# Attention, experts and a gated matrix product on one core: tiles at multiples of 64 bytes, an earlier split of w_out, and three loads that move

## The chip, the cores and the metric

The kernel runs on one core of a Trainium2 chip. The metric is device time in microseconds (us). The kernel before was run three times: 1268.51, 1266.70 and 1268.42 us, median 1268.42.

## The reference, cut to what matters

```python
# attention: 4 batches, 8 heads, 576 rows, 64 wide; keys and values pooled by 8
attn = softmax(scale * q @ mean8(k).T);  x = attn @ mean8(v)      # x: 2304 x 512
# experts: all 4 for every row, weighted by p
for e in range(4):
    out += p[:, e] * (relu(x @ w1[e]) @ w2[e])                    # w1: 512 x 1024, w2: 1024 x 512
# gated product
a, b = x @ w1, x @ w2                                             # x is the experts' out
h = (a * b) @ w3;  result = h @ w_out                             # w3: 1024 x 1024, w_out: 1024 x 512
```

All is in fp32. The kernel splits every operand of a large product into a high and a low part (`hi_lo`, L115: ScalarE copies the rounded high part, VectorE or GpSimd subtracts it) and makes each product from three matmuls (`mm3`, L110: lines 111, 112, 113).

## The kernel before

**Stages.** A lead-in and the attention share the first 200 us with the first expert. Then come the experts: 4 experts by 6 blocks of 384 rows by 8 slices of the hidden width, 192 units. A unit makes one slice of the hidden layer, `expert_h` (12 matmuls "g1", x moves over w1), and two units later (LAG = 2) that slice's share of the output (12 matmuls "g2", the slice `hh`, `hl` moves over w2). After the last slice of a block, `accumulate` multiplies the four sums with p on VectorE and adds them on GpSimd.

**The w3 stage** uses the same loop with 24 more units, numbered n = 0 to 23 in `made` (blocks of 3, 3 and 2 row tiles by 8 slices). It multiplies w3 with w_out beforehand, so that the last stage needs one product. `w3_h` takes a slice of w3 from the stream and splits it into the same tiles `hh`, `hl` (here the stationary operand), and 9 (in the last block 6) matmuls of 512 columns move w_out over it. `keep_w34` splits the sums at the end of a block. Between the units `made` prepares the next stage: `weights_of(j, 0)` and `(j, 1)` make the seven combinations of the gate weights of column block j, `prepare_x` those of the rows of batch 0, `put_away` stores these operands in DRAM.

**The last stage** goes twice ("halves" of the width) over 4 batches. For each of four j, `gated_rows` makes seven products of 12 matmuls of 288 columns and multiplies the two results; then 4 or 5 row tiles of 12 matmuls each go over the kept w3 w_out ("w34"). The operand of a batch has two slots, kc = 0 and 1. In the second half they are loaded from DRAM (`fetch_x`), kc = 0 into a spare slot during the products, kc = 1 (`next_x(1, first)`, L1019) into the slot that the products have just read. At the swap of the halves (`swap`: first half, batch 3) four new `weights_of` are made, two at L975 before the w34 tiles and two between them.

**What sets the order.** All is issued by hand in program order, and each engine and the one DMA queue (SP's) work in that order. `Stream` holds four raw tiles and issues a load when one is taken; `take` and `split` block SP until the raw tile is free. In the w3 stage the stream carries w_out, w3 and the gate weights, in the order written in `stream_last`.

```python
822  n = key[0] * FC + fc
823  if n + 3 < FC: stream.split(nc.vector)             # w_out, slices 3 to 7
831  if n in (7, 10, 13, 16): weights_of((n - 7) // 3, 0)
833  if n in (8, 11, 14, 17): weights_of((n - 8) // 3, 1)
837  if n in (9, 15): prepare_x(n // 15, slot(), kept_d[0][n // 15])
```

The first three slices of w_out are split at the end of the last expert block (L817 to 820), since `wo` shares the pool "z", which takes the place of the experts' tiles.

**Addresses.** Tiles lie in two stacks, from the left and from the right end of each partition. In the program before, the right stack ends 32 bytes past a multiple of 64. The tiles `hh`, `hl` (also as w3's) and `xo` (the batch operand's regular slots) are in the right stack and begin 32 bytes past a multiple of 64. The tiles of x, w1, w2, w34, z (w_out, the gated rows `g`, and the spare slots, which go under the name g too) and of the gate weights (`wh`, `wl`) are in the left one and begin at multiples of 64.

Of the kernel before, what the change touches and what calls it, by code (L numbers as in the profile page):

```python
# [17 lines left out]
def fused_kernel(  # L18
# [21 lines left out]
    nc = tc.nc  # L40
# [40 lines left out]
    xpool = experts.enter_context(tc.tile_pool(name="xpool", bufs=NB))  # L81
    w1pool = experts.enter_context(tc.tile_pool(name="w1pool", bufs=FC))
    ppool = ctx.enter_context(tc.tile_pool(name="ppool", bufs=1, side="right"))
    hpool = ctx.enter_context(tc.tile_pool(name="hpool", bufs=LAG + 1, side="right"))
    dpool = ctx.enter_context(tc.tile_pool(name="dpool", bufs=1, space=bass.MemoryType.DRAM))
    ps_q = ctx.enter_context(tc.tile_pool(name="ps_q", bufs=1, space=PSUM))
# [177 lines left out]
    with tc.manual_schedule():  # L264
# [225 lines left out]
        def probs():  # L490
            sp = ap.tile([P, NTILE], F32, tag="sp", name="sp", bufs=1)
            nc.vector.tensor_reduce(sp, dp, axis=AX.X, op=ALU.add)
            nc.vector.tensor_scalar(sp, sp, 1e-9, None, op0=ALU.add)
            nc.vector.reciprocal(sp, sp)
            nc.vector.tensor_tensor(dp, dp, sp.unsqueeze(2).broadcast_to([P, NTILE, E]), op=ALU.mult)
# [78 lines left out]
        def load_p(e, i):  # L574

            pb = ppool.tile([P, TPB, P], F32, tag="p", name="p")
            rows = p_d.rearrange("(t e) s -> e t s", e=E)[e, i * TPB:(i + 1) * TPB]
            nc.sync.dma_start(pb, rows.unsqueeze(0).broadcast_to([P, TPB, P]))
            p_t[e, i] = pb.rearrange("p t s -> p (t s)")
# [49 lines left out]

        parts = {}  # L630

        def weights_of(j, n=None):

            def split(src, at, m, eng):
                src = src.rearrange("p a b c -> p (a b c)") if len(src.shape) == 4 else src.rearrange("p a c -> p (a c)")
                hi_lo(*(t[:, at:at + m].rearrange("p a b c -> p (a b c)") for t in wop_t[j]), src, eng)

            if n != 1:
                (left, _), (right, _) = stream.take(2)
                wop_t[j] = tuple(late["wops"].tile([P, 7, 2, P], F32R, tag=t, name=t) for t in ("wh", "wl"))  # L640
                s = parts[j] = late["small"].tile([P, 4, 2, P], F32, tag="t", name="s", bufs=1)
                sub, add = ALU.subtract, ALU.add
                nc.vector.tensor_tensor(s[:, 0], right[:, :2], right[:, 2:], op=add)
                nc.vector.tensor_tensor(s[:, 1], s[:, 0], left[:, :2], op=sub)
                nc.vector.tensor_tensor(s[:, 2], left[:, :2], right[:, :2], op=sub)
                nc.vector.tensor_tensor(s[:, 3], left[:, 2:], s[:, 1], op=sub)
                split(left, A11, 2, nc.vector)
                split(right[:, 2:], A22, 1, nc.vector)
                stream.fill()
            if n != 0:  # L650
                split(parts.pop(j), S1, 4, nc.gpsimd)
# [15 lines left out]
        def prepare_x(kc, to, keep, n=None):  # L667

            (bh, th), (bl, tl) = to
            if n in (None, 0):  # L670
                r = xr_t.pop(kc)
                t = late["small"].tile([P, 4, HB], F32, tag="t", name="t", bufs=1)
                sub = ALU.subtract
# [17 lines left out]
        def put_away():  # L691
            for f in stores:
                f()
            stores.clear()
# [63 lines left out]
        def enter_wide():  # L758

            experts.close()  # L760
            for name, bufs in (("z", FC), ("wops", NJ), ("small", 1)):
                late[name] = ctx.enter_context(tc.tile_pool(name=name, bufs=bufs, reuse_waits="tile"))

        def enter_operands():
            assert rounding.finished()
            later.close()
            late["xo"] = ctx.enter_context(tc.tile_pool(name="xo", bufs=4, side="right", reuse_waits="tile"))

# [26 lines left out]
        def made(u):  # L795

            kind, key, fc = u
            if kind == "e":
                e, i = key
                if e == 0 and i == 0:  # L800
                    if fc + LAG < FC:
                        stream.split(nc.vector)
                    stream.split()
                if i == NB - 1 and e < E - 1:
                    stream.split()
# [4 lines left out]
                if e == E - 1:  # L810
# [6 lines left out]
                    if i == NB - 1 and fc == FC - 1:  # L817
                        enter_wide()
                        for _ in range(3):
                            stream.split(nc.vector)  # L820
            else:
                n = key[0] * FC + fc
                if n + 3 < FC:
                    stream.split(nc.vector)
                if n == LAG + 1:
                    store_acc(NB - 1)
                if n == LAG + 2:
                    enter_operands()
                    for kc in range(2):
                        load_x(acc_d, 0, kc)  # L830
                if n in (7, 10, 13, 16):
                    weights_of((n - 7) // 3, 0)
                if n in (8, 11, 14, 17):
                    weights_of((n - 8) // 3, 1)
                if n in (13, 19):
                    put_away()
                if n in (9, 15):
                    prepare_x(n // 15, slot(), kept_d[0][n // 15])

# [32 lines left out]
        def stream_last():  # L872
            def make(fc):
                def dst():
                    t = late["z"].tile([P, 2, 1, DM], F32R, tag="z", name="wo")
                    wo_t[fc] = t[:, 0], t[:, 1]
                    return wo_t[fc]
                stream.add([late["wo"][fc]], (1, DM), dst)

            for fc in range(3):  # L880
                make(fc)
            for n, (b, fc) in enumerate((b, fc) for b in range(len(w3_blocks)) for fc in range(FC)):
                t0, rn = w3_blocks[b]
                stream.add([late["w3"][fc * P:(fc + 1) * P, t0 * P:(t0 + rn) * P]], (1, rn * P), rn)
                if n + 3 < FC:
                    make(n + 3)
                if n in (7, 10, 13, 16):
                    add_gates(0, (n - 7) // 3)

# [33 lines left out]

        half_d = [dpool.tile([P, DM], F32, tag=f"half{t}", name=f"half{t}") for t in range(NTILE)]
        z_t = [late["z"].tile([P, 2, S], F32R, tag="z", name="g") for _ in range(FC)]
        g_t = z_t[:NJ]
# [21 lines left out]
        for half in range(2):  # L948
            for b in range(B):
# [22 lines left out]
                lead_in = S % P if b % 2 else 0  # L972
                tiles = []
                if swap:
                    weights_of(0)  # L975
                    weights_of(1)
                first = b * S - (S % P if b % 2 else 0)
                if b % 2:
                    tiles.append((first // P, lambda j: edge[:, j]))
                for m in range(S // P):  # L980
# [36 lines left out]
                earlier(1)  # L1017
                first, second = xo_t[0], xo_t[1]
                next_x(1, first)  # L1019
                if half == 0 and b < B - 2:  # L1020
# [50 lines left out]
```

## Time and profile before

| | |
|---|---|
| three runs | 1268.51, 1266.70, 1268.42 us |
| the profiled execution's own time | 1272.72 us |
| its span, first to last instruction | 1271.0 us |
| mean granted TensorE clock | 0.981 of full |
| w3 stage, from its first to the last stage's first matmul | 910.22 to 975.33 us |
| swap of the halves, first matmul that waits | 1120.22 us |

The profile is one execution with each instruction's start and duration. "PE" is TensorE's matmuls; their durations overlap, so the distance between starts tells the pace. "DVE" is VectorE, "ACT" ScalarE, "POOL" GpSimd, "SPq" the issuing of DMAs. In brackets stands how long the engine had been idle and what released it.

### The profile page before, as it was taken

What the parts mean: (1) busy time and instruction counts of PE and PEld (TensorE: products, weight loads), DVE (VectorE), ACT (ScalarE), POOL (GpSimd) and SP (SyncE); (2) the same over time, 40 slices, a digit from 0 to 9 for tenths busy, and PEclk for the clock granted to TensorE, in tenths of its full rate; (3) what the DMA queues carried; (4) which work ended last, traced back from release to release, by engine and by line L of the source; (5) the groups of instructions that cost most, each with busy time, mean ns of one, the idle gap of its engine ahead of it and who ended that gap; (6) DMA issues with size and microseconds to landing.
All of it is one profiled execution on the core that took longest, in us unless ns stands there. A gap on an engine that the chain in (4) does not pass through costs nothing.

```text
span 1271.0 us, 18785 instructions
## 1 busy us (share of the span) xinstructions
PE 1222.8 (96%) x7089; PEld 1166.4 (92%) x7089; DVE 663.6 (52%) x1497; ACT 276.3 (22%) x535; POOL 358.5 (28%) x424
## 2 busy tenths in 40 slices
PE   6899999999999999999999999999978999989997
PEld 5788898999999999999999999999856999979996
DVE  4777544444445456444443544444465777655453
ACT  3343331122111113111113111111343333221010
POOL 4574410034122236212216421212121222331121
PEclk9799999999999999999999999999988999989999
DMA  7753201143112235222124322222355343755531
GB/s 178 184 161 109 57 7 57 44 129 104 56 46 57 57 98 148 57 57 57 55 59 131 93 72 78 73 77 87 112 166 186 120 181 139 256 199 196 210 136 66
DMA packets 147758, 138.47 MB, mean 109 GB/s; under 512 B 48524, under 2 KB 114644, under 8 KB 147668
## 3 DMA queue, kind: packets, MB, share of 16 engines
q1 hardware_dynamic: 147668, 137.28, 35.2%
q8 instruction: 55, 0.90, 0.3%
q14 instruction: 35, 0.29, 0.1%
HBM read 96.05 MB, written 41.19 MB: 108 GB/s over the span
## 4 chain that ended last, share of the span: by engine, by line
PE 88%; DMA 4%; DVE 4%; issue 1%; POOL 1%; SPq 1%; ACT 1%; DVEq 0%; POOLq 0%; ACTq 0%
PE g L111 24%; PE g L112 23%; PE g L113 23%; PE s L111 5%; PE s L112 5%; PE s L113 5%; PE x_ps L445 1%; PE sc L399 1%; PE at_ps L433 1%; DMA raw<-gate 1%; DMA xol<-kept 1%; DMA stxl<-in_v_dram 1%; DMA raw<-wo 0%; DVE kp L331 0%; DMA stxh<-in_q_dram 0%
## 5 line engine op out<-in xcount | busy, mean ns | idle before, releaser
L571 DVE SCALAR_TENSOR_TENSOR hhl<-g,hhh 128x384 fp32r<-128x384 f32 x192 | 106.6, 556 | 369.3 <-ACT hhh L570 369.2
L111 PE MATMUL g<-xl,w1h 128*128 128x384 f32 x768 | 263.6, 343 | 1.0 <-DVE xl L117 1.0
L111 PE MATMUL g<-hhl,w2h 128*128 128x384 f32 x768 | 262.4, 342 | 0.2 <-DVE part L590 0.2
L113 PE MATMUL g<-hhh,w2h 128*128 128x384 f32 x768 | 260.0, 339 | 0.0
L112 PE MATMUL g<-hhh,w2l 128*128 128x384 f32 x768 | 260.0, 339 | 0.0
L112 PE MATMUL g<-xh,w1l 128*128 128x384 f32 x768 | 259.8, 338 | 0.0
L113 PE MATMUL g<-xh,w1h 128*128 128x384 f32 x768 | 259.2, 338 | 0.0
L570 ACT ACTIVATE hhh<-g 128x384 fp32r<-128x384 f32 x192 | 94.7, 493 | 589.9 <-PE g L113 539.8
L223 POOL TENSOR_TENSOR dtmp<-dtmp 128x256 f32<-128x256 f32 x80 | 58.9, 736 | 412.5 <-DVE dtmp L222 367.0
L111 PEld LDWEIGHTS g<-xl,w1h 128*128 128x128 f32 x768 | 145.2, 189 | 6.0 <-DVE xl L117 2.3
L111 PEld LDWEIGHTS g<-hhl,w2h 128*128 128x128 f32 x768 | 144.1, 188 | 4.9 <-issue 4.0
L112 PEld LDWEIGHTS g<-xh,w1l 128*128 128x128 f32 x768 | 145.5, 189 | 0.0
L113 PEld LDWEIGHTS g<-xh,w1h 128*128 128x128 f32 x768 | 145.2, 189 | 0.0
L113 PEld LDWEIGHTS g<-hhh,w2h 128*128 128x128 f32 x768 | 144.2, 188 | 0.0
L112 PEld LDWEIGHTS g<-hhh,w2l 128*128 128x128 f32 x768 | 144.1, 188 | 0.0
L117 POOL TENSOR_TENSOR g<-c,g 128x576 fp32r<-128x576 f32 x32 | 47.5, 1484 | 206.4 <-ACT g L116 206.4
L591 POOL TENSOR_TENSOR acc<-acc,part 128x384 f32<-128x384 f32 x72 | 71.0, 1020 | 103.7 <-DVE part L590 103.7
L111 PE MATMUL s<-xol,wh 128*128 128x288 f32 x308 | 92.0, 299 | 6.3 <-DMA xol<-kept 6.3
L112 PE MATMUL s<-xoh,wl 128*128 128x288 f32 x308 | 91.9, 298 | 0.0
L113 PE MATMUL s<-xoh,wh 128*128 128x288 f32 x308 | 90.6, 294 | 0.0
L111 PEld LDWEIGHTS s<-xol,wh 128*128 128x128 f32 x308 | 58.3, 189 | 7.3 <-DMA xol<-kept 6.8
L113 PEld LDWEIGHTS s<-xoh,wh 128*128 128x128 f32 x308 | 58.8, 191 | 0.0
(137 smaller groups left out, 1756.0 us busy)
## 6 DMA issues: line engine op xcount, KB each, us to landing
raw<-in_moe_w_dram SPq DMA_DIRECT2D x64, 256.0 KB
din<-in_moe_w_dram SPq DMA_DIRECT2D x64, 256.0 KB
p<-p SPq DMA_DIRECT2D x24, 192.0 KB
acc<-acc SPq DMA_DIRECT2D x6, 768.0 KB
xr<-acc SPq DMA_DIRECT2D x16, 288.0 KB
half<-ob SPq DMA_DIRECT2D x18, 256.0 KB
half<-half SPq DMA_DIRECT2D x18, 256.0 KB
out_dram<-half SPq DMA_DIRECT2D x18, 256.0 KB
```

The lines of the kernel that those rows point to most:

```text
L111: nc.tensor.matmul(ps, lh, rl, start=first, stop=False)
L112: nc.tensor.matmul(ps, ll, rh, start=False, stop=False)
L113: nc.tensor.matmul(ps, lh, rh, start=False, stop=last)
L117: (lo_eng or nc.vector).tensor_tensor(lo, src, hi.bitcast(F32), op=ALU.subtract)
L223: nc.gpsimd.tensor_tensor(a, a, b, op=ALU.add)
L399: nc.tensor.matmul(sc[off:off + n, (hp % 2) * W:(hp % 2 + 1) * W], qT[:, hp, off:off + n], kT_t[b][:, hp * W:(hp + 1) * W], start=True, st ...
L433: nc.tensor.transpose(pt[:NK, g * P:(g + 1) * P], e[:, half * G + g, :], ident)
L445: nc.tensor.matmul(px[a * D:(a + 1) * D, off:off + n], vp_t[b][:NK, 2 * hp + a], at_t[i, hp // 2][:NK, 2 * (hp % 2) + a, off:off + n], sta ...
L570: nc.scalar.activation(hh, ps, AF.Relu)
L571: nc.vector.scalar_tensor_tensor(hl, ps, 0.0, hh.bitcast(F32), op0=ALU.max, op1=ALU.subtract)
L591: nc.gpsimd.tensor_tensor(acc_t[i][:, c], acc_t[i][:, c], part, op=ALU.add)
```

## The change

- `ppool`'s tile and `sp` get 8 more floats, of which the kernel uses none. The right stack's tiles then begin at multiples of 64.
- `w1pool` moves from the left to the right stack (`firsts`) and lives on through the w3 stage. The eight slices of w_out are split into its tiles, one in each unit of the last expert block (`stream.split()`, low part on GpSimd), as w1's tiles come free.
- "z" is opened after the w3 stage, on the right; `xo` moves to the left.
- The gate weights of the first half leave the stream. `load_gates(j)` loads them into tiles of tag "c" at n = 1, 6, 12, 17.
- `weights_of(j, 0)` stands at n = 5, 11, 16, 19, `weights_of(j, 1)` at 6, 12, 18, 20. `prepare_x` goes in three pieces at n = 7, 8, 10 and 13, 14, 15; `load_x` moves from n = 4 to 0, `put_away` from 13, 19 to 14, 18.
- The scratch tag "t" has two buffers instead of one.
- `next_x(1, first)` stands ahead of the swap's `weights_of(0)`, and so also ahead of `earlier(0)`, `earlier(1)` (the loads of the first half's sums).

```diff
-    w1pool = experts.enter_context(tc.tile_pool(name="w1pool", bufs=FC))
+    firsts = ctx.enter_context(ExitStack())
+    w1pool = firsts.enter_context(tc.tile_pool(name="w1pool", bufs=FC, side="right"))
-            sp = ap.tile([P, NTILE], F32, tag="sp", name="sp", bufs=1)
+            sp = ap.tile([P, NTILE + 8], F32, tag="sp", name="sp", bufs=1)[:, :NTILE]
-            pb = ppool.tile([P, TPB, P], F32, tag="p", name="p")
+            pb = ppool.tile([P, TPB * P + 8], F32, tag="p", name="p")[:, :TPB * P].rearrange("p (t s) -> p t s", s=P)
+        def load_gates(j):
+            gate_t[j] = [late["small"].tile([P, KC, P], F32, tag="c", name="gate", bufs=3) for _ in gates_d]
+            for r, d in zip(gate_t[j], gates_d):
+                nc.sync.dma_start(r, d[:, j * P:(j + 1) * P].rearrange("(k p) f -> p k f", p=P))
-                (left, _), (right, _) = stream.take(2)
+                left, right = gate_t.pop(j) if j in gate_t else (r for r, _ in stream.take(2))
-                s = parts[j] = late["small"].tile([P, 4, 2, P], F32, tag="t", name="s", bufs=1)
+                s = parts[j] = late["small"].tile([P, 4, 2, P], F32, tag="t", name="s", bufs=2)
-            late["xo"] = ctx.enter_context(tc.tile_pool(name="xo", bufs=4, side="right", reuse_waits="tile"))
+            late["xo"] = ctx.enter_context(tc.tile_pool(name="xo", bufs=4, reuse_waits="tile"))
-                if i == NB - 1 and e < E - 1:
+                if i == NB - 1:
                     stream.split()
...
-                        for _ in range(3):
-                            stream.split(nc.vector)
...
+                if n == 0:
+                    for kc in range(2):
+                        load_x(acc_d, 0, kc)
...
+        early = {n: [lambda j=j: load_gates(j)] for j, n in enumerate((1, 6, 12, 17))}
+        for j, (one, two) in enumerate(((5, 6), (11, 12), (16, 18), (19, 20))):
+            early.setdefault(one, []).append(lambda j=j: weights_of(j, 0))
+            early.setdefault(two, []).append(lambda j=j: weights_of(j, 1))
+        for kc, steps in enumerate(((7, 8, 10), (13, 14, 15))):
...
+        for n in (14, 18):
+            early[n].append(put_away)
...
+            for fc in range(FC):
+                add_rows(late["wo"][fc], w1pool, "w1", wo_t, fc)
+            for t0, rn in w3_blocks:
+                for fc in range(FC):
+                    stream.add([late["w3"][fc * P:(fc + 1) * P, t0 * P:(t0 + rn) * P]], (1, rn * P), rn)
...
+        firsts.close()
+        late["z"] = ctx.enter_context(tc.tile_pool(name="z", bufs=FC, side="right", reuse_waits="tile"))
...
+                first, second = xo_t[0], xo_t[1]
+                next_x(1, first)
                 if swap:
                     weights_of(0)
                     weights_of(1)
...
                 earlier(0)
                 earlier(1)
-                first, second = xo_t[0], xo_t[1]
-                next_x(1, first)
```

## Rows read from the trace of the kernel before

**Rows 1.** The page's first section: the span.

```profile
span 1271.0 us, 18785 instructions
```

**Rows 2.** The page's chain that ended last, shares of the span by engine.

```profile
PE 88%; DMA 4%; DVE 4%; issue 1%; POOL 1%; SPq 1%; ACT 1%; DVEq 0%; POOLq 0%; ACTq 0%
```

**Rows 3.** Busy time by stretch; columns: length, PE, PEld, DVE, ACT, POOL, clock, DMA.

```profile
400.00:500.00 100.00, 100.00 (x570) 100.00 (x569) 50.95 (x126) 19.91 (x38) 35.34 (x36) 1.00 0.35 89
910.22:975.33 65.11, 51.55 (x192) 39.34 (x193) 40.03 (x72) 26.66 (x49) 13.86 (x8) 0.84 0.62 204
911.59:914.96 3.37, 3.37 (x9) 2.48 (x8) 2.96 (x5) 1.04 (x2) 2.78 (x3) 0.50 0.10 31
915.22:928.57 13.35, 13.35 (x58) 10.73 (x57) 4.27 (x9) 3.72 (x8) 0.00 (x0) 1.00 0.88 283
938.38:942.31 3.93, 3.92 (x9) 3.17 (x10) 3.90 (x9) 1.56 (x4) 0.00 (x0) 0.50 0.16 50
962.90:966.20 3.30, 3.29 (x8) 2.62 (x9) 1.91 (x4) 0.93 (x3) 1.19 (x1) 0.50 0.39 132
997.68:1008.63 10.95, 10.95 (x50) 9.01 (x49) 10.32 (x16) 4.55 (x9) 4.10 (x4) 1.00 0.03 6
1120.20:1126.66 6.46, 6.04 (x23) 5.70 (x24) 1.76 (x5) 1.56 (x3) 2.36 (x1) 0.50 1.01 365
```

**Rows 4.** Timeline of PE: first matmul of two g1 groups and the g2 between.

```profile
895.07 0.34 PE L111 MATMUL g<-xl,w1h 128*128 128x384 f32 x1
...
897.17 0.34 PE L111 MATMUL g<-hhl,w2h 128*128 128x384 f32 x1
...
899.29 0.34 PE L111 MATMUL g<-xl,w1h 128*128 128x384 f32 x1
```

**Rows 5.** Groups by line and shape, whole span: count, busy us, mean ns, idle before.

```profile
L113 PE MATMUL s<-xoh,wh 128*128 128x288 f32 x308 | 90.6, 294 | 0.0
L113 PE MATMUL s<-g,wh 128*128 128x288 f32 x140 | 41.6, 297 | 0.0
L117 POOL TENSOR_TENSOR w2l<-raw,w2h 128x512 fp32r<-128x512 f32 x32 | 41.2, 1294 | 14.7 <-ACT w2h L116 11.2 <-issue 3.3 <-POOL kb L332 0.2
L117 DVE TENSOR_TENSOR w3hl<-raw,w3hh 128x256 fp32r<-128x256 f32 x8 | 3.4, 422 | 7.5 <-ACT w3hh L116 7.5
```

**Rows 6.** Timeline of PE: the w3 stage's three stops, where it goes on.

```profile
910.22 0.48 PE L111 MATMUL g<-wo,w3hh 128*128 128x512 f32 x1 [2.30 <-DVE part L590]
...
938.39 0.80 PE L111 MATMUL g<-wo,w3hh 128*128 128x512 f32 x1 [6.68 <-DVE w34l L117]
...
962.91 0.80 PE L111 MATMUL g<-wo,w3hh 128*128 128x512 f32 x1 [4.80 <-DVE w34l L117]
```

**Rows 7.** Timeline of VectorE ahead of the first two stops.

```profile
908.92 0.69 DVE L117 TENSOR_TENSOR wo<-raw,wo 128x512 fp32r<-128x512 f32 x1 [1.01 <-ACT wo L116]
...
927.96 0.43 DVE L643 TENSOR_TENSOR s<-raw 128x256 f32<-128x256 f32 x1 [4.17 <-DMA raw<-gate]
...
930.37 3.18 DVE L117 TENSOR_TENSOR w3hl<-raw,w3hh 128x384 fp32r<-128x384 f32 x2
933.48 0.45 DVE L674 TENSOR_TENSOR t<-xr 128x288 f32<-128x288 f32 x1
...
937.66 1.88 DVE L117 TENSOR_TENSOR w34l<-g,w34h 128x512 fp32r<-128x512 f32 x3
```

**Rows 8.** Timeline of GpSimd at the same time.

```profile
930.68 2.45 POOL L117 TENSOR_TENSOR wl<-s,wh 128x1024 fp32r<-128x1024 f32 x1 [16.31 <-ACT wh L116]
```

**Rows 9.** Timeline of the DMA queue at the swap of the halves.

```profile
1105.18 7.00 SPq L136 DMA_DIRECT2D raw<-gate  x4
1112.27 0.93 SPq L699 DMA_DIRECT2D xoh<-kept  x2
```

**Rows 10.** Timeline of PE at the swap.

```profile
1114.06 0.29 PE L113 MATMUL s<-g,wh 128*128 128x288 f32 x1
1120.22 0.61 PE L111 MATMUL s<-xol,wh 128*128 128x288 f32 x1 [5.87 <-DMA xol<-kept]
```

More of the change, by code (lines that the diff above doesn't have):

```diff
@@ L628, in fused_kernel @@
         B11, B21, B22, T1, T2, T3, T4 = range(7)
-        parts = {}
+        parts, gate_t = {}, {}
+        def load_gates(j):
+            gate_t[j] = [late["small"].tile([P, KC, P], F32, tag="c", name="gate", bufs=3) for _ in gates_d]
+            for r, d in zip(gate_t[j], gates_d):
+                nc.sync.dma_start(r, d[:, j * P:(j + 1) * P].rearrange("(k p) f -> p k f", p=P))
         def weights_of(j, n=None):
@@ L671, in prepare_x @@
                 r = xr_t.pop(kc)
-                t = late["small"].tile([P, 4, HB], F32, tag="t", name="t", bufs=1)
+                t = late["small"].tile([P, 4, HB], F32, tag="t", name="t", bufs=2)
                 sub = ALU.subtract
@@ L760, in enter_wide @@
             experts.close()
-            for name, bufs in (("z", FC), ("wops", NJ), ("small", 1)):
+            for name, bufs in (("wops", NJ), ("small", 1)):
                 late[name] = ctx.enter_context(tc.tile_pool(name=name, bufs=bufs, reuse_waits="tile"))
@@ L818, in made @@
                         enter_wide()
-                        for _ in range(3):
-                            stream.split(nc.vector)
             else:
                 n = key[0] * FC + fc
-                if n + 3 < FC:
-                    stream.split(nc.vector)
+                if n == 0:
+                    for kc in range(2):
+                        load_x(acc_d, 0, kc)
                 if n == LAG + 1:
@@ L828, in made, with piece @@
                     enter_operands()
[L829 to L838, printed above, removed]
+                for f in early.get(n, ()):
+                    f()
+        early = {n: [lambda j=j: load_gates(j)] for j, n in enumerate((1, 6, 12, 17))}
+        for j, (one, two) in enumerate(((5, 6), (11, 12), (16, 18), (19, 20))):
+            early.setdefault(one, []).append(lambda j=j: weights_of(j, 0))
+            early.setdefault(two, []).append(lambda j=j: weights_of(j, 1))
+        places = {}
+        for kc, steps in enumerate(((7, 8, 10), (13, 14, 15))):
+            for m, n in enumerate(steps):
+                def piece(kc=kc, m=m):
+                    if m == 0:
+                        places[kc] = slot()
+                    prepare_x(kc, places[kc], kept_d[0][kc], m)
+                early.setdefault(n, []).append(piece)
+        for n in (14, 18):
+            early[n].append(put_away)
         def met(u):
@@ L872, in stream_last @@
         def stream_last():
[L873 to L888, printed above, removed]
+            for fc in range(FC):
[3 more added lines that the diff above has]
+                    stream.add([late["w3"][fc * P:(fc + 1) * P, t0 * P:(t0 + rn) * P]], (1, rn * P), rn)
         hs, pss = {}, None
@@ L976, in fused_kernel @@
                     weights_of(1)
-                first = b * S - (S % P if b % 2 else 0)
                 if b % 2:
-                    tiles.append((first // P, lambda j: edge[:, j]))
+                    tiles.append(((b * S - S % P) // P, lambda j: edge[:, j]))
                 for m in range(S // P):
```

## The prediction, made before the changed kernel was run

> **What bounds the kernel now.** The page's chain comes first: of 1271.0 us [rows 1] TensorE holds 88% [rows 2]. So an edit pays only where it lets TensorE stand less, run at the higher clock, or issue its matmuls closer. The stretches say where that is possible [rows 3]. From 400 to 500 us, amid the experts, PE is busy throughout at clock 1.00, with 570 matmuls: nothing stands there, only the pace could change. The w3 stage, 910.22 to 975.33, is another matter: 192 matmuls in 65.11 us, of which PE is busy 51.55, at a mean clock of 0.84. The timeline of PE shows the large stops and who ended them [rows 6]: 2.30 us until VectorE's first expert product was through, 6.68 and 4.80 us until it had split the block's sums (`w34l`). After each, PE issues at half the pace with clock 0.50 (the 1.2 GHz level) for 3.37, 3.93 and 3.30 us [rows 3]. The one other large stop is the swap of the halves: 5.87 us until the operand had landed [rows 10], then 6.46 us at 0.50 [rows 3].
>
> **Why VectorE was late.** Its timeline has the cause [rows 7]. It works in program order, and what PE waits for is queued behind work that is due much later. Before the first stop it stands at a split of w_out whose data came late (908.92). Before the second it waits 4.17 us for gate weights, until 927.96; then come `weights_of` (2.4 us, 927.96 to 930.37), two splits of w3 (3.18), the whole of `prepare_x` (4.2 us, 933.48 to 937.66), and only then the `w34l` that frees PE's banks. The third stop repeats this with n = 15, 16 and 17.
>
> **The w3 stage, term by term.** It takes 2.30 + 65.11 = 67.4 us. Its matmuls alone: in the undisturbed stretch 915.22 to 928.57, 57 start (the 58th row began before it), so one each 234 ns; the w34 tiles, also 512 columns, start 48 in 10.95 us, one each 228 ns [rows 3]. In the first the stationary operand is off the multiple of 64, in the second it is on it. Nothing else that I see sets them apart, so I take 228 after the change: 192 x 0.228 = 43.8 us. At 234 it would be 44.9; this edit is worth 0 to 1.2 us.
>
> Stop one: no split of w_out is left ahead of the expert products. Their banks are complete one after the other while PE still works on the last slice, so VectorE follows close behind, and w3's first slices were loaded in the last expert block. I take 0 for the stop, at most 1.2.
>
> Stops two and three: n = 7 and 9 now have no more than 2.4 us of preparation each. A unit takes PE 9 x 0.228 = 2.1 us and `w3_h` runs two units ahead, so a piece of 2.4 us fits into the lead. I take 0 at n = 9. From n = 16 the blocks have two tiles and a unit lasts 1.4 us. There VectorE has two pieces of 2.4, one of 1.9 (`w34l`) and five splits of w3 of 0.42 [rows 5]: 8.8 us, while PE does units 14 to 18 in 2 x 2.1 + 3 x 1.4 = 8.4 and the lead is short. I take 1.7 us of stop, between 0 and 4.8 (today's).
>
> The DMA queue: `load_x` and `load_gates` now come early and stand between the loads of w3, and `load_gates(1)` to `(3)` make SP wait for a tile of the `weights_of` before. `put_away` (2 MB) comes at n = 14 and 18, ahead of the last slices of w3. Each raw tile is asked for three units ahead, 6 us in the first blocks and 4 us in the last. I take 1.5 us for the last slices, between 0 and 6.
>
> Sum: 43.8 + 1.7 + 1.5 = 47.0 us, so 67.4 - 47.0 = **20.4 us** saved, which holds if the short stops do not pull the clock down; one such stretch costs half of 3.3 to 3.9 us [rows 3].
>
> **The last expert block** takes over eight splits: a copy on ScalarE and 1.29 us on GpSimd each [rows 5], one in a unit of 24 matmuls, 4.2 us [rows 4]. ScalarE must wait for the first load, a few us, with the next slice's `hh` behind it; the lead of two units, 8.4 us, hides that. If it did not, PE would stand for the rest. I take 0, at most 3 us.
>
> **The swap.** SP sends the operand's load at 1112.27, behind four gate loads that it began to send at 1105.18 and that took it 7.00 us, since they wait for raw tiles [rows 9]. It lands 8 us later [rows 10]. Sent first, it can go when the last product has read its slot, ahead of the 60 w34 matmuls of 0.228, thus 13.7 us before 1114.06. It then lands near 1108.4 and the stop is gone, with its slow stretch: 5.87 + 6.46 / 2 = **9.1 us**. The gate loads go out behind it, and the second buffer of "t" lets VectorE prepare the next `weights_of` while GpSimd works on the last. What could be late next is these weights: the third is needed two `gated_rows` later, and four took 22.35 us, 975.33 to 997.68, where the stretches of [rows 3] end and begin. Lower end 6 us, if that fails.
>
> In the other batches of the second half the loads of the sums (`earlier`) now queue behind 2 MB. With 4 row tiles, w34 lasts 10.9 us, and the load (8 us by the swap's) with two sums of 0.26 MB behind it needs about 9 to 10. I take 0, at worst 3 us over the batches; free banks of PE stand in between.
>
> **The pace of g2.** Its moving operand `hh`, `hl` gets aligned. A g1 group, with aligned operands, takes 2.10 us; the g2 group after it 2.12 [rows 4]; rounded rows, so 0.01 to 0.03 apart. Over 192 groups that is 1.9 to 5.8 us if alignment is all of it, and 0 if it is the order of banks. The products speak for little: `xo`, off the multiple, has 294 ns, the aligned spare slot (named g) 297 [rows 5]. I take **1.5 us** for g2, 0 for `xo`.
>
> The aligned g1 starts a matmul each 2.10 / 12 = 175 ns, although 384 columns at 2.4 GHz are 160 ns [rows 4]. The Trainium skill ("TensorE: Matmul & The Clock Gate", section "Back-to-back issue gap") gives N / 2.4 + 2.5 ns for a matmul by itself, so 162.5 ns here, and says that weight loads alter it in a stream; aligned g1 doesn't reach that figure.
>
> **Sum.** 20.4 + 9.1 + 1.5 = 31.0 us. The profiled execution took 1272.72 us, 1241.7 after; the median of the runs, 1268.42, lies 4.3 us lower: **1237.4 us**.
>
> **Rivals.**
> (a) VectorE or the w3 loads stay late, and the stage keeps half its loss. For it: in the second chain w3's splits took 3.18 us for two, while GpSimd's 2.45 us operation ran [rows 7, 8]; four such operations remain, and each may hold VectorE for up to its 2.45 us (9.8 in all), with slow clock behind the stops. Against it: the chain is broken up. Time: 1237.4 + 10.2 = 1247.6. The Trainium skill ("SBUF — State Buffer", section "SBUF: two separate sides") states this as a lock: a VectorE operation with two SBUF inputs waits while GpSimd holds the shared port pair, for its whole instruction. The 3.18 us agree; by it all four would hold.
> (b) The distance over 160 ns in g2 is all misalignment: (2.12 / 12 - 0.160) x 2304 = 38 us go, in place of 1.5, thus 1201. Against it: aligned g1 has nearly the same distance. By the page on TensorE quoted above the gain would be 14 ns x 2304 = 32 us.
> (c) The sums' loads behind the operand delay the second half, and the swap gives only 6: 1237.4 + 3 + 3.1 = 1243.5.
> (d) Slower: w1 on the right. If the 6 ns between w3 and w34 belong to a stationary operand in the right stack and not to the 32 bytes, all 2304 matmuls of g1 pay. At 6 ns that is 13.8 us, and w3 keeps its 1.2: time 1252; from 31 / 2304 = 13.5 ns on the kernel is no faster, and at twice that 31 us slower, 1299. For it: w3 is the only stationary operand of 512-column matmuls that lay there. Against it: no row shows a matmul over 6 ns dearer for its operand's place.
>
> **How the numbers follow.** Forecast 0.66, (a) 0.20, (b) 0.03, (c) 0.05, (d) 0.06, half of it past the point where it decides. The forecast's own range is 1232 to 1244. The range takes in (a) and (c) and the bounds: at the low end no stop left and g2's 5.8 us (1237.4 - 3.2 - 4.3 = 1230), at the high end (a) with the lower end of the swap and no gain in g2 (1247.6 + 3.1 + 1.5 = 1252): 1229 to 1253. A measurement tells 0.2%, 2.5 us, from no change. Faster by more: 0.95; within: 0.02; slower: 0.03, from (d).
>
> **What would show it.** Right: 192 w3 matmuls in about 47 us at a clock near 1.00, no stop over 2 us on `w34l`, none on `kept` at the swap, 228 ns a w3 matmul, g2 groups as long as g1's. Wrong: stops on `w3hl` or `w34l` from n = 16 on, ScalarE waiting for raw w3, g1 groups over 2.11 us, or VectorE's sums waiting longer for `half`.

## The result, and the profile after

The changed kernel takes 1237.45 us (median of four runs, 1236.21 to 1239.93), the one before 1268.47 beside it: a ratio of 0.9757, interval 0.9735 to 0.9779. That is 31.0 us less; the prediction was 1237.4. The profiled execution took 1237.02. The total came out where the sum put it, but not every term did, as the stretches show.

The page of the changed kernel, its span and its chain by engine:

```profile
span 1235.0 us, 18786 instructions
...
PE 87%; DVE 5%; DMA 3%; issue 1%; POOL 1%; ACT 1%; SPq 1%; DVEq 0%; POOLq 0%; ACTq 0%
```

TensorE still sets the end [rows 2]. The span is 36.0 us shorter [rows 1], the medians 31.0: 4.35 us of the difference arose before the last attention matmul (200.69 us before, 196.34 after), ahead of the stages that the change was to shorten, and the profiles of the other kernels below reach that point between 195.3 and 199.0. So the starts of PE's matmuls are compared by stretch, and that first one is left out:

```
stretch (PE's starts)                          before   after   saved   predicted
experts, to the last g2 matmul                 706.89  701.38     5.5         1.5
from there to the last w3 matmul's successor    67.75   48.91    18.8        20.4
first half, to the swap's first product        138.47  139.32    -0.9           0
products after the swap                         31.72   22.59     9.1         9.1
rest                                           125.5   126.46    -1.0           0
sum (of the unrounded savings)                                   31.7        31.0
```

Busy time of the changed kernel by stretch (columns as in [rows 3], with GB/s at the end): amid the experts; the w3 stage; its part without a stop; the first w34 matmuls; the products after the swap.

```profile
400.00:500.00 100.00, 100.00 (x575) 100.00 (x574) 53.66 (x131) 21.14 (x40) 37.70 (x38) 1.00 0.38 96
897.90:946.63 48.73, 45.25 (x193) 35.59 (x193) 40.76 (x69) 25.84 (x47) 13.80 (x8) 1.00 0.76 251
915.98:931.87 15.89, 15.89 (x72) 13.14 (x70) 15.63 (x29) 10.35 (x19) 2.50 (x1) 1.00 0.67 222
968.88:980.09 11.21, 11.21 (x51) 8.99 (x49) 10.43 (x16) 4.81 (x9) 4.16 (x4) 1.00 0.05 8
1085.95:1108.54 22.59, 22.49 (x170) 22.25 (x168) 17.61 (x37) 7.34 (x14) 9.97 (x8) 1.00 0.36 133
```

Beside [rows 3]: 575 matmuls in 100 us amid the experts where there were 570; a w3 stage of 48.73 us at clock 1.00 instead of 65.11 at 0.84; the products after the swap at 1.00. In the third line 70 matmuls start in 15.89 us, 227 ns each, where w3 had 234. But in the fourth, w34's 48 starts take 11.21 us, 233.5 ns each, where they had 228. The w3 pace and the w34 pace have changed places.

PE's timeline of the changed kernel: the end of the last expert product, the first w3 matmul, and every stop of the w3 stage.

```profile
897.72 0.34 PE L114 MATMUL g<-hhh,w2h 128*128 128x384 f32 x1
897.90 0.40 PE L112 MATMUL g<-w1l,w3hh 128*128 128x512 f32 x1
...
915.64 0.50 PE L112 MATMUL g<-w1l,w3hh 128*128 128x512 f32 x1 [0.37 <-DVE w34l L118]
...
933.11 0.50 PE L112 MATMUL g<-w1l,w3hh 128*128 128x512 f32 x1 [0.85 <-DVE w34l L118]
...
937.31 0.50 PE L113 MATMUL g<-w1h,w3hl 128*128 128x512 f32 x1 [0.28 <-DVE w3hl L118]
...
940.05 0.50 PE L113 MATMUL g<-w1h,w3hl 128*128 128x512 f32 x1 [1.08 <-DVE w3hl L118]
...
942.61 0.50 PE L113 MATMUL g<-w1h,w3hl 128*128 128x512 f32 x1 [0.91 <-DVE w3hl L118]
```

The first of the three old stops [rows 6] is gone; the others have shrunk to five small ones. From start to start they cost 0.53, 1.01, 0.44, 1.24 and 1.06 us, 4.3 in all, and no slow clock follows. VectorE's and GpSimd's timelines show whose the last three are:

```profile
909.12 2.29 DVE L118 TENSOR_TENSOR w3hl<-raw,w3hh 128x384 fp32r<-128x384 f32 x1 [0.38 <-ACT w3hh L117]
...
922.02 2.52 DVE L118 TENSOR_TENSOR w3hl<-raw,w3hh 128x384 fp32r<-128x384 f32 x1 [0.16 <-ACT w3hh L117]
...
934.17 0.41 DVE L118 TENSOR_TENSOR w3hl<-raw,w3hh 128x256 fp32r<-128x256 f32 x1
934.84 2.42 DVE L118 TENSOR_TENSOR w3hl<-raw,w3hh 128x256 fp32r<-128x256 f32 x1 [0.25 <-ACT w3hh L117]
...
939.58 0.42 DVE L118 TENSOR_TENSOR w3hl<-raw,w3hh 128x256 fp32r<-128x256 f32 x1
940.15 2.40 DVE L118 TENSOR_TENSOR w3hl<-raw,w3hh 128x256 fp32r<-128x256 f32 x1 [0.16 <-ACT w3hh L117]
```

```profile
908.51 2.49 POOL L118 TENSOR_TENSOR wl<-s,wh 128x1024 fp32r<-128x1024 f32 x1 [6.58 <-ACT wh L117]
921.63 2.50 POOL L118 TENSOR_TENSOR wl<-s,wh 128x1024 fp32r<-128x1024 f32 x1 [10.63 <-ACT wh L117]
934.58 2.40 POOL L118 TENSOR_TENSOR wl<-s,wh 128x1024 fp32r<-128x1024 f32 x1 [10.46 <-ACT wh L117]
939.89 2.38 POOL L118 TENSOR_TENSOR wl<-s,wh 128x1024 fp32r<-128x1024 f32 x1 [2.91 <-ACT wh L117]
```

A split that takes 0.41 us takes 2.42 when GpSimd has begun its 2.40 us operation just before, and ends 0.28 us after it. The stops at 937.31 and 942.61 end as such a split ends (937.26 and 942.55). The one at 940.05 ends with a split of 0.42 us that stood in VectorE's queue behind gate weights, which VectorE could begin only once the first of the two was through (937.18). This is rival (a) at work, at 0.28 + 1.08 + 0.91 us of stop and not at 9.8. All four of GpSimd's operations held a split, which took 2.29 to 2.52 us (0.41 or 0.55 alone); behind the first two (909.12 and 922.02), in blocks with longer units, PE did not stop for a split. The Trainium skill ("SBUF — State Buffer", section "SBUF: two separate sides") calls the pair of ports that GpSimd and VectorE share an exclusive lock, held for the whole instruction. The trace agrees: 0.41 alone, 2.42 beside it.

At the swap, the DMA queue of the changed kernel:

```profile
1071.77 0.80 SPq L706 DMA_DIRECT2D xoh<-kept  x2
1072.61 0.91 SPq L706 DMA_DIRECT2D xol<-kept  x2
...
1076.99 5.39 SPq L137 DMA_DIRECT2D raw<-gate  x4
```

The operand now goes first, 14 us ahead of the products (1085.95), and the gate loads behind it wait in its place [rows 9]. PE has no stop there. The price expected on VectorE is there too. Its waits for the first half's sums in the kernel before, from 1126 us on, and in the changed one, from 1100 us on (us in all, times, longest):

```profile
DVE half L1005 <- DMA half<-half: 16.0, 9, 2.9
```

```profile
DVE half L1011 <- DMA half<-half: 24.9, 11, 7.0
```

The longest wait grew from 2.9 to 7.0 us. After none of the eleven does PE stop: rival (c) has its mechanism and no price.

### The profile page after: what moved, and what is told of

The parts are those of the page before. It is cut to its first block, busy times and chain, and to the rows that moved or that the text cites. A ratio compares the mean times of both kernels' runs of the same rounds, so it can differ in the third digit from the quotient of the medians.

```text
span 1235.0 us, 18786 instructions
## 1 busy us (share of the span) xinstructions
PE 1207.5 (98%) x7089; PEld 1151.8 (93%) x7089; DVE 666.8 (54%) x1489; ACT 276.3 (22%) x535; POOL 369.0 (30%) x432
## 4 chain that ended last, share of the span: by engine, by line
PE 87%; DVE 5%; DMA 3%; issue 1%; POOL 1%; ACT 1%; SPq 1%; DVEq 0%; POOLq 0%; ACTq 0%
PE g L112 23%; PE g L113 23%; PE g L114 23%; PE s L112 5%; PE s L114 5%; PE s L113 5%; PE x_ps L446 1%; PE at_ps L434 1%; PE sc L400 1%; DMA stxl<-in_v_dram 1%; DVE w3hl L118 1%; DVE kp L332 1%; DMA stxh<-in_v_dram 1%; DVE s L651 1%; DMA half<-half 0%
## 5 line engine op out<-in xcount | busy, mean ns | idle before, releaser
L113 PEld LDWEIGHTS s<-xoh,wl 128*128 128x128 f32 x308 | 57.9, 188 | 0.2
```

What stands on the lines that cost most here:

```text
L113: nc.tensor.matmul(ps, ll, rh, start=False, stop=False)
```

## The experiments

Two questions were left. **The paces**: g2 gained 3 ns a matmul, w3 gained 7, w34 lost 6, and the multiple of 64 explains the first two at most. **The stops**: is each removed stop owed to the part of the change to which the prediction gave it? The theory for the stops was the prediction's. For the paces it was a multiple of 64 for either operand; the rivals were the stack (left or right) in which an operand lies, a larger multiple, and the distance between the two operands.

A matmul's pace is taken from start to start: for g1 and g2 the median over the groups of 12 after 250 us, for w3 the median of single steps at full clock, for w34 the median over its groups. Where the operands lay is the remainder of their addresses by 128, moving operand first, stationary second. The traces do not show addresses; the remainders follow from the order and the sizes of the tiles in the two stacks.

```
kernel        g1             g2             w3             w34
before        (0,0)   175.7  (96,0)  176.5  (0,96)  234    (0,0)  227.2
after         (0,64)  175.9  (64,0)  173.5  (64,64) 227    (0,64) 233.0
align_alone   (0,0)   175.4  (64,0)  172.9  (0,64)  234    (0,0)  227.5
z_128         (0,64)  176.0  (64,0)  173.5  (64,64) 227    (0,0)  227.2
x_64          (64,64) 175.2  (64,0)  173.7  (64,64) 227    (0,64) 233.0
x_64_w1_0     (64,0)  173.3  (64,0)  173.3  (0,64)  234    (0,64) 233.0
all_128       (0,0)   173.3  (0,0)   173.3  (0,0)   227    (0,0)  227.2
before_128    (0,0)   173.3  (0,0)   173.3  (0,0)   227    (0,0)  227.0
```

**1. The two paddings alone, in the kernel before.**

```diff
-            sp = ap.tile([P, NTILE], F32, tag="sp", name="sp", bufs=1)
+            sp = ap.tile([P, NTILE + 8], F32, tag="sp", name="sp", bufs=1)[:, :NTILE]
-            pb = ppool.tile([P, TPB, P], F32, tag="p", name="p")
+            pb = ppool.tile([P, TPB * P + 8], F32, tag="p", name="p")[:, :TPB * P].rearrange("p (t s) -> p t s", s=P)
```

> The kernel before with the two paddings alone, so that hh, hl, w3's tiles and xo begin at multiples of 64 bytes; nothing else moves. Theory 1 (the 32 bytes are what g2 and w3 paid): g2 groups fall from 176.5 to 173.5 ns a matmul, as in the changed kernel, w3 from 234 to 227, together 2304 x 3.0 + 192 x 7 = 8.3 us, near 1260. Theory 2 (the pace follows where the other tiles lie): g2 and w3 stay near 176 and 234 ns, under 2 us, near 1267. The stops of the w3 stage and of the swap stay under both.

Measured 1260.11 us (1268.79 for the kernel before, beside it), ratio 0.9937 (0.9914 to 0.996). The experts take 699.15 us instead of 706.89. Stretches of this kernel, amid the experts and in the w3 stage:

```profile
400.00:500.00 100.00, 100.00 (x576) 100.00 (x575) 54.16 (x132) 20.51 (x39) 38.00 (x39) 1.00 0.38 96
902.35:917.27 14.92, 14.92 (x65) 12.03 (x64) 6.69 (x10) 4.33 (x8) 2.25 (x2) 1.00 0.76 240
```

576 matmuls in 100 us: g2's gain is the padding. But w3, whose stationary operand now lies at a multiple of 64, starts 64 in 14.92 us, 233 ns each. The 7 ns that w3 gained are not what the prediction took them for.

**2. The operand's load first, in the kernel before.**

```diff
+                slot0, second = xo_t[0], xo_t[1]
+                next_x(1, slot0)
                 if swap:
                     weights_of(0)
...
-                first, second = xo_t[0], xo_t[1]
-                next_x(1, first)
```

> The kernel before with the operand's load ahead of the swap's weights, alone. Theory 1 (the load was late because it was sent late): the stop of 5.9 us at the swap and the slow stretch behind it go, 9.1 us, near 1259.3. Theory 2 (the gate loads, now behind 2 MB, make the weights late instead): a stop on the new weights comes in its place, over 3 us, near 1263 or later.

Measured 1261.66 us, ratio 0.9949 (0.9933 to 0.9965). The products after the swap take 24.62 us instead of 31.72: 7.1 of the 9.1 us. PE's timeline there:

```profile
1117.85 0.40 PE L111 MATMUL s<-g,wh 128*128 128x288 f32 x1 [2.05 <-ACT ob L1010]
```

The operand is no longer waited for, but one stop of 2.05 us is left, on ScalarE's copy of an output bank. No slow clock follows it (the stretch 1111 to 1140 has 1.00).

**3. One buffer of "t", in the changed kernel.**

```diff
-                s = parts[j] = late["small"].tile([P, 4, 2, P], F32, tag="t", name="s", bufs=2)
+                s = parts[j] = late["small"].tile([P, 4, 2, P], F32, tag="t", name="s", bufs=1)
-                t = late["small"].tile([P, 4, HB], F32, tag="t", name="t", bufs=2)
+                t = late["small"].tile([P, 4, HB], F32, tag="t", name="t", bufs=1)
```

> The changed kernel with one buffer of tag t instead of two. Theory 1 (what the load sent first alone left of the swap's stop, 2.1 us on the output copies, is the weights' chain through this one tile): a stop of about 2 us at the swap returns, and in the w3 stage the weights wait for GpSimd, 2 to 4 us in all, near 1240.5. Theory 2 (the tile is free in time when the load goes first): no change over 1 us.

Measured 1240.18 us, ratio 0.9764 (0.9748 to 0.978), 1270.57 for the kernel before, beside it: by the ratios the time is not told apart from the changed kernel's. The trace is clearer. The stop of run 2 is back:

```profile
1095.82 0.40 PE L112 MATMUL s<-g,wh 128*128 128x288 f32 x1 [1.72 <-ACT ob L1014]
```

The products after the swap take 24.23 us instead of 22.59. The w3 stage, where part of the loss was expected, loses nothing (48.50 us, 48.73 in the changed kernel). So the swap's 9.1 us are two things: about 7 for the load, and about 2 for the second buffer, without which the next weights, and ScalarE behind them, come late.

**4. `prepare_x` in one piece, in the changed kernel.**

```diff
-        for kc, steps in enumerate(((7, 8, 10), (13, 14, 15))):
+        for kc, steps in enumerate(((9, 9, 9), (15, 15, 15))):
-            early[n].append(put_away)
+            early.setdefault(n, []).append(put_away)
```

> The changed kernel with prepare_x in one piece at n = 9 and 15, as before the change; all else stays. Theory 1 (the stops were VectorE's queue): at n = 9 the sums of the first block wait behind 4.2 us of prepare_x again, and at n = 15 to 17 behind 4.2 + 2.4 us; PE stands some 2 to 3 us more at each and the clock may fall, 4 to 8 us in all, 1241 to 1245. Theory 2 (the gates' and w_out's loads were what made VectorE late): with these gone the whole piece fits, under 1.5 us, near 1238.

Measured 1242.33 us, ratio 0.9799 (0.9776 to 0.9823). PE's timeline, and the stretches behind its two stops:

```profile
918.50 0.80 PE L112 MATMUL g<-w1l,w3hh 128*128 128x512 f32 x1 [3.27 <-DVE w34l L118]
...
938.97 0.80 PE L112 MATMUL g<-w1l,w3hh 128*128 128x512 f32 x1 [2.27 <-DVE w34l L118]
```

```profile
918.45:921.87 3.42, 3.37 (x8) 2.72 (x9) 1.66 (x3) 0.35 (x1) 0.00 (x0) 0.50 0.17 48
938.93:942.35 3.42, 3.38 (x8) 2.71 (x9) 3.10 (x7) 1.24 (x3) 1.65 (x1) 0.50 1.00 368
```

The old stops return at half their size, each with 3.4 us at the 1.2 GHz level behind it. The stage takes 53.32 us, 4.6 more. Cutting `prepare_x` is worth that. The rest of the old stops (6.68 and 4.80 us [rows 6]) is then owed to the other edits in the stage, by the prediction's account to the gate weights' own loads; that part was not run by itself, so it is argued and not shown.

**5. w_out split back in the w3 stage, in the changed kernel.**

```diff
-                if i == NB - 1:
+                if i == NB - 1 and e < E - 1:
                     stream.split()
...
+                        for _ in range(3):
+                            stream.split(nc.vector)
...
+                if n + 3 < FC:
+                    stream.split(nc.vector)
```

(The loads of w_out and w3 alternate again, as before.)

> The changed kernel with w_out split where it was before: three slices at the end of the last expert block, five in the first units of the w3 stage, on VectorE, its loads between those of w3. Theory 1 (a late load of w_out held VectorE ahead of the expert products): the stop of 2.3 us at the start of the stage and the slow clock behind it (1.7 us) return, 4 us, near 1241.5. Theory 2 (the gate weights are what counted): no stop at the start over 0.5 us, near 1238.

Measured 1241.85 us, ratio 0.9795 (0.9774 to 0.9816). The first stop is back, with 3.4 us at clock 0.50 behind it:

```profile
902.82 0.48 PE L112 MATMUL g<-w1l,w3hh 128*128 128x512 f32 x1 [2.38 <-DVE part L592]
```

```profile
903.37:906.80 3.43, 3.43 (x10) 2.69 (x9) 2.60 (x4) 0.00 (x0) 3.43 (x4) 0.50 1.00 323
```

From the last g2 start to the first w3 start it is 2.72 us instead of 0.18, and the stage takes 2.0 us more: 4.5 us for this part. In the changed kernel the eight splits in the last expert block cause no stop (each of ScalarE's copies there takes 0.62 to 0.63 us, one every 4.2 us).

**6. 64 bytes on the right, ahead of z: its tiles go to a multiple of 128.**

```diff
+        zpad = ctx.enter_context(tc.tile_pool(name="zpad", bufs=1, side="right"))
+        zpad.tile([P, 16], F32, tag="zpad", name="zpad")
         late["z"] = ...
```

> The changed kernel with 64 bytes of padding ahead of the pool z, so that the gated rows begin at multiples of 128 bytes as in the kernel before; they stay in the right stack. Theory 1 (w34 lost its pace, 228 to 233.4 ns, because stationary and moving operand now differ by 64 bytes modulo 128): w34 goes back to 228 ns, 432 x 5.4 = 2.3 us, near 1235. Theory 2 (it is the place in the right stack): 233 ns stay, 1237.4.

Measured 1235.63 us, ratio 0.9742 (0.9722 to 0.9762). The time alone isn't told apart from the changed kernel's; the pace is. The first w34 matmuls:

```profile
969.83:980.76 10.93, 10.93 (x51) 8.97 (x50) 10.22 (x16) 4.54 (x9) 4.17 (x4) 1.00 0.03 4
```

48 starts in 10.93 us, 227.7 ns. z still lies in the right stack, so the stack is not the cause of w34's loss; the 64 bytes are.

**7. 64 bytes ahead of x.**

```diff
+    xpad = experts.enter_context(tc.tile_pool(name="xpad", bufs=1))
+    xpad.tile([P, 16], F32, tag="xpad", name="xpad")
```

> The changed kernel with 64 bytes of padding ahead of the pool of x, so that g1's moving operand begins 64 bytes past a multiple of 128, as g2's does, and as its stationary w1 does too. Theory 1 (the pace is best where both operands have the same offset modulo 128): g1 stays near 175.7 ns, as before the change with both at 0, no change over 1 us. Theory 2 (a moving operand at 64 modulo 128 is cheaper whatever the other): g1 falls to 173.5, 2304 x 2.4 = 5.5 us, near 1232. Theory 3 (the place decides): no change.

Measured 1237.63 us, ratio 0.9756 (0.9734 to 0.9777). With both g1 operands 64 off, g1 has 175.2 ns, little less than 175.9. What the median over a group hides is told below.

**8. 64 bytes ahead of x, and 64 ahead of w1: w1 goes to a multiple of 128.**

```diff
+    xpad = experts.enter_context(tc.tile_pool(name="xpad", bufs=1))
+    xpad.tile([P, 16], F32, tag="xpad", name="xpad")
...
+    wpad = firsts.enter_context(tc.tile_pool(name="wpad", bufs=1, side="right"))
+    wpad.tile([P, 16], F32, tag="wpad", name="wpad")
```

> The changed kernel with x at 64 and w1 at 0 modulo 128 bytes, so g1 has the offsets that g2 has (moving 64, stationary 0), and the w3 stage moves w_out at 0 over w3 at 64. Theory 1 (384 columns are fastest at moving 64, stationary 0; 512 columns pay 6 to 7 ns wherever the two offsets differ): g1 falls from 175.9 to 173 ns, 2304 x 2.9 = 6.7 us, and w3 goes from 227 to 234, 1.3 us back: near 1232. Theory 2 (g2 is faster for another reason than these offsets, such as its four banks): g1 stays at 175 to 176, and the time at 1238.

Measured 1232.86 us, ratio 0.9723 (0.9703 to 0.9743). g1 falls to 173.3 ns with w1 in the right stack, at (64,0). But w3, at (0,64) again, rises to 234, although nothing of its work was changed: its moving operand lies in w1's old tiles. Amid the experts:

```profile
400.00:500.00 100.00, 100.00 (x579) 100.00 (x578) 53.44 (x131) 21.14 (x41) 38.37 (x39) 1.00 0.38 96
```

**9. Everything at a multiple of 128, in the changed kernel.**

```diff
-            pb = ppool.tile([P, TPB * P + 8], F32, tag="p", name="p")[:, :TPB * P].rearrange("p (t s) -> p t s", s=P)
+            pb = ppool.tile([P, TPB * P + 24], F32, tag="p", name="p")[:, :TPB * P].rearrange("p (t s) -> p t s", s=P)
```

> The changed kernel with 24 instead of 8 floats of padding in ppool's tile, so that every operand begins at a multiple of 128 bytes. Theory 1 (512 columns pay where the two offsets differ modulo 128; 384 are fastest at moving 64, stationary 0): w34 goes from 233 to 227.5 ns (2.4 us gained), w3 stays at 227, g2 loses its place and rises from 173.5 to 175.5 (4.6 us lost): near 1239.7. Theory 2 (multiples of 128 are best for all): g2 stays at 173.5 or below, 1235.

Measured 1230.54 us, ratio 0.9703 (0.9681 to 0.9725). g1, g2, w3 and w34 all have the lowest pace that their kind shows in these kernels, but for 0.4 ns of g2 in run 1. g2 did not rise, so theory 1 is wrong; and neither theory had the gain of g1, so the time is 4.5 us under the lower of the two. 579 matmuls in 100 us:

```profile
400.00:500.00 100.00, 100.00 (x579) 100.00 (x578) 54.15 (x132) 21.16 (x40) 38.24 (x38) 1.00 0.37 96
```

**10. The same, and w1 at a multiple of 2048 bytes from x.**

```diff
+    wpad = firsts.enter_context(tc.tile_pool(name="wpad", bufs=1, side="right"))
+    wpad.tile([P, 192], F32, tag="wpad", name="wpad")
```

> all_128 with 768 bytes of padding ahead of w1pool, so that w1 still begins at multiples of 128 bytes on the right, but lies a multiple of 2048 bytes from x, as it did in the kernel before. Theory 1 (in the kernel before, g1 had 175.7 ns with both operands at multiples of 128 because of this distance): g1 goes from 173.3 to 175.5, 5 us, near 1235.6. Theory 2 (the left stack cost it, or what else is there): g1 stays at 173.3, near 1230.5.

Measured 1231.03 us, ratio 0.9691 (0.9677 to 0.9706), g1 at 173.3 ns as in run 9: this distance between the operands makes no difference.

**11. Everything at a multiple of 128, in the kernel before.** The edit of run 1 with 24 floats in place of 8 in `pb`; w1 stays on the left.

> The kernel before with the two paddings alone, ppool's tile padded by 24 floats, so that every operand begins at a multiple of 128 bytes with w1 still on the left. Theory 1 (all that counts is that both operands begin at multiples of 128): g1 and g2 both go to 173.3 ns, w3 to 227, together 2304 x (2.4 + 3.2) + 192 x 7 = 14.2 us, near 1254.5. Theory 2 (w1 on the left costs g1 2 ns whatever the offsets): g1 stays near 175.5, g2 goes to 173 and w3 to 227, 8.9 to 9.4 us, near 1259.5.

Measured 1258.2 us (1270.93 for the kernel before, beside it), ratio 0.9904 (0.9886 to 0.9922). The experts take 696.16 us instead of 706.89, and w3 has 227 ns:

```profile
400.00:500.00 100.00, 100.00 (x579) 99.92 (x578) 53.35 (x131) 21.13 (x41) 38.15 (x39) 1.00 0.37 96
897.99:912.54 14.55, 14.55 (x66) 12.01 (x64) 6.70 (x10) 4.36 (x8) 2.26 (x2) 1.00 0.78 247
```

64 starts in 14.55 us, 227.3 ns. The paces of run 9 are had in the old kernel, with w1 on the left. g1's operands lie here exactly as before, at (0,0), and g1 still gains 2.4 ns: only g2's moving operand has come to a multiple of 128. The paces are those of theory 1, but the time is not its 1254.5: the experts' stretch holds some 2000 matmuls of g1 and of g2 each and not 2304, and the w3 stage is no shorter for its pace (65.77 us, 65.11 before), since its stops are still there.

**12. The better version: run 9, with the two late GpSimd operations of the w3 stage after it.**

```diff
-        for j, (one, two) in enumerate(((5, 6), (11, 12), (16, 18), (19, 20))):
+        for j, (one, two) in enumerate(((5, 6), (11, 12), (16, 23), (19, 23))):
-            early[n].append(put_away)
+            early.setdefault(n, []).append(put_away)
```

> The changed kernel with all operands at multiples of 128 bytes (as in all_128) and weights_of(2, 1) and (3, 1) at n = 23, behind the last split of w3, instead of 18 and 20. Theory 1 (the last three stops of the w3 stage are w3's splits, which take 2.4 instead of 0.4 us while GpSimd makes these parts): the stops at 0.65, 1.47 and 1.28 us go, 2.7 us less than all_128, near 1227.8. Theory 2 (VectorE has too much to do there whatever GpSimd does): the stops stay or move to the sums at the end of the stage, near 1230.5.

Measured 1229.54 us (four runs, 1228.43 to 1230.81; 1270.57 before), ratio 0.9682 (0.9667 to 0.9696). This beats both kernels, the changed one by 0.77% by the ratios; from run 9 the time does not tell it apart. VectorE's last splits of w3 in it, and PE's stops:

```profile
936.21 0.42 DVE L118 TENSOR_TENSOR w3hl<-raw,w3hh 128x256 fp32r<-128x256 f32 x1 [3.30 <-ACT w3hh L117]
936.82 0.42 DVE L118 TENSOR_TENSOR w3hl<-raw,w3hh 128x256 fp32r<-128x256 f32 x1 [0.18 <-ACT w3hh L117]
```

```profile
926.45 0.50 PE L112 MATMUL g<-w1l,w3hh 128*128 128x512 f32 x1 [0.83 <-DVE w34l L118]
...
932.63 0.50 PE L113 MATMUL g<-w1h,w3hl 128*128 128x512 f32 x1 [0.90 <-DVE w3hl L118]
...
936.23 0.51 PE L112 MATMUL g<-w1l,w3hh 128*128 128x512 f32 x1 [0.81 <-ACT w3hh L117]
```

```profile
935.76 0.42 ACT L117 ACTIVATE w3hh<-raw 128x256 fp32r<-128x256 f32 x1 [4.99 <-DMA raw<-w]
```

The last splits are held no more (an earlier one, at 915.38, still takes 2.49 us and stops nothing). But the stage takes 47.78 us, 0.65 less than in run 9 (48.43) and not the 2.7 less that were expected: stops of 0.90 and 0.81 us stand in place of the old. ScalarE now waits 4.99 us for the last raw w3, so the loads are the next thing late: the DMA queue, on which PE did not stand in the changed kernel, costs 0.81 us of the prediction's 1.5 here. In runs 9 and 12 the swap has a stop again, of 0.66 and 0.69 us, on ScalarE's copies of output banks.

## Why the prediction was right, and where its sum was not

- **The w3 stage** (20.4 predicted, 18.8 measured). The three stops fell as worked out. Run 5 brings the first back, and run 4 the other two at half their size, so two of the causes named are shown and the gate weights' part is not. The stops left were mis-sized: 1.7 us for the last block and 0 at n = 7 and 9, where 4.3 came up in all: 0.5 after the first block (915.64), 1.0 after the second (933.11) and 2.7 in the three stops behind GpSimd's last operations. The 1.5 us for the DMA queue did not come up on PE. The 0.8 us that are left lie in the matmuls right behind the stops and at the start of the stage, up to 340 ns each. None of the stops was followed by slow clock, as the sum had assumed.
- **w3's pace** (234 to 228). The size was right: 192 matmuls x 7 ns are 1.3 us, in the bounds of 0 to 1.2 but for a tenth. The cause was wrong: the multiple of 64 for the stationary operand does nothing by itself (run 1 has 234 ns at (0,64)). The gain came by luck: the move of w_out into w1's old tiles put the moving operand 64 off too, like the stationary one. The step that failed is "Nothing else that I see sets them apart": the two groups compared also stood on and off the multiple of 128, and where the moving operand would lie after the change was not looked at.
- **g2's pace** (1.5 us). The term that was mis-sized: 176.5 to 173.5 ns is 3.0 ns for each of the 2016 g2 matmuls that start after the attention, 6.0 us, a little over even the upper bound of 5.8 (with g1's 0.2 ns lost, near the 5.5 of the table). The prediction judged g2 against the aligned g1 and took that for the floor. But g1 was itself slow: its 175.7 fell to 173.3 when g2's operand moved to a multiple of 128 (run 11).
- **w34's pace** (not in the sum). Its 432 matmuls took 2.4 us longer than before. z was put on the right, 64 off; run 6 gives the pace back. This is more than the 1.8 us that the first half and the rest lost in the table. The prediction put the term at nothing without a reason: it did not ask what z's new place would do to the matmuls that read it.
- **The swap** (9.1, measured 9.1): right, with about 2 us of it owed to the second buffer (runs 2 and 3).
- **The rivals.** (a) happened: all four operations held VectorE, at a quarter of the price on PE; (c) only on VectorE. (b) is refuted: the lowest group median of a 384-column matmul in any kernel here is 172.9 ns, the steady pace 173.3. By the formula of the Trainium skill ("TensorE: Matmul & The Clock Gate", section "Back-to-back issue gap") for a matmul by itself the estimate is 162.5 ns; measured, with weight loads in between, are 173.3. (d) is refuted by runs 8 and 9, where w1 lies on the right and g1 is fastest. Its suspicion was near the mark all the same: the move did put g1 at (0,64), where it has 2.6 ns more than in run 9. It paid only 0.2 of them because at (0,0) it already paid 2.4 for another reason, which is luck.

Against the sum, the experts gave 4.0 us more, the w3 stage 1.6 less, and the first half and the rest, with w34 in them, 1.8 less: the mechanisms of the stops were right, but that the total came out so close is in part luck, since errors cancelled.

## What to carry to other kernels

Put both operands of every matmul in a dense stream of fp32r matmuls at multiples of 128 bytes: here 64 was not enough at 384 and 512 columns (at 288 no difference was seen), and a group could pay for its neighbour's operand. Before you give a difference in pace to one property, list the addresses of both operands in every group that you compare. Where an engine in program order holds up TensorE, cut its early work into pieces shorter than the lead, and keep GpSimd's long two-input operations out of the stretch in which VectorE has the last word.

## What the runs showed of the hardware that was not expected

**Operand addresses set the pace.** At full clock, a 512-column matmul took 227 ns at (0,0) and (64,64), and 233 to 234 at (0,64) or (0,96); a 384-column one 173 ns at (0,0), (64,0) and (64,64) once the first steps of its group are over, and about 176 at (0,64) or (96,0). No kernel has 512 columns at (64,0). The 288-column products had 132 to 133 in every kernel. The weight loads had 188 to 189 ns in the changed kernel's g1 and g2 alike.

**A group pays for the step from other offsets.** The twelve steps of a group, in ns, each the median over the groups:

```
before, g1       (0,0) after (96,0)   176 171 175 177 185 176 182 173 173 173 173 173
align_alone, g1  (0,0) after (64,0)   172 171 175 177 185 176 182 173 174 173 173 174
x_64, g1         (64,64) after (64,0) 185 176 182 173 174 173 173 173 173 173 173 173
after, g1        (0,64) after (64,0)  170 178 176 177 176 178 176 177 176 178 176 174
all_128, g1      (0,0) after (0,0)    173 173 174 173 173 174 173 173 174 173 173 174
```

At (0,0) and (64,64) the first steps after a change of offsets are slow, the later ones at 173; at (0,64) all are slow; with nothing changing none is. That is how g1 gained in run 11 without being moved. Why (0,64) costs and (64,0) does not, and what the first steps wait for, was not settled: these runs show the pattern, not its cause.

**Stops and the clock.** The stops of 2.27 and 3.27 us in run 4 and of 2.38 us in run 5 were each followed by 3.4 us at the 1.2 GHz level, like those of 2.30 us and more in the kernel before [rows 3, 6]; the one of 2.05 us in run 2, the one of 1.72 in run 3 and all of the changed kernel's w3 stops were not.
